# One product of 512 columns, which nobody reads, ahead of each group of transposes in a kernel of chunked attention and routed feed-forward

## The chip, the cores and the metric

The kernel runs on one core of a Trainium2 chip. The metric is the device time of one execution in microseconds; several executions are timed, and their median counts. One more execution is recorded by the hardware profiler. The engines are named as in the profile: PE is TensorE's matmul, PEld its loading of weights, DVE is VectorE, ACT is ScalarE, POOL is GpSimd and SP is SyncE, which issues DMAs.

## The reference

Two stages follow each other. The first is attention in chunks of 32 rows over a sequence of 768, for 4 batches of 8 heads with 64 features each. A chunk sees its own 32 keys, 16 to the left, 8 to the right, and 8 keys of a memory:

```python
for c in range(nc):                      # 24 chunks of 32
    q_c   = q[:, :, c_start:c_end]
    k_ctx = k[:, :, max(0, c_start - 16):min(S, c_end + 8)]
    k_full = np.concatenate([mem_k, k_ctx], axis=2)     # v_full alike
    scores = scale * np.matmul(q_c, k_full.transpose(0, 1, 3, 2))
    a = softmax(scores)
    out[:, :, c_start:c_end] = np.matmul(a, v_full)
```

The second takes the heads side by side as 512 features. For each batch it picks the 128 rows of 768 with the highest `x @ w_gate`, and adds a gated feed-forward result to these rows alone:

```python
top_idx = np.argpartition(-scores[b], capacity)[:capacity]
xe = x[b, top_idx]
ye = np.maximum(xe @ w1, 0.0) @ w2
out[b, top_idx] = x[b, top_idx] + g[:, None] * ye       # g: sigmoid of the scores
```

## The kernel before

The work is cut into 16 pairs of heads (4 for each batch) and 4 batches of routing. Each piece is a step with a name, a number and an engine: `TK.3.p` is step TK of pair 3 on TensorE (`p`), `.v` is VectorE, `.a` ScalarE, `.g` GpSimd, `.s` SyncE. The string ORDER at the top of the file lists all steps in one order, written out by hand; the last loop of the kernel walks through it and issues them. Each engine carries out its own steps in that order and waits by semaphores for what a step needs. There is no scheduler behind it.

The steps of a pair, as far as they are spoken of here:

- LK, LQ, LV (line 141) load K, Q and V of a pair from memory, with a cast from float32 to float16, as DMAs that GpSimd issues. MK and MV (lines 157 and 163) copy the rows of the memory keys and values in, from SyncE; those of pair 0 come from GpSimd (155, 161). Six buffers for each of K, Q and V go round, so the load of pair n + 6 waits until the transposes of pair n have read theirs.
- TK, TQ and TV (function `tr`, line 269) transpose these tiles on TensorE: 16 products for each step, into one PSUM bank. Four banks (pool `prr`) go round for all steps that use `bank16` or `bank32`. There are 16 x 3 = 48 of these groups.
- EK, EQ, EV (copies at lines 127 to 131) bring the result to kT, qT and vT; FK, FV and VP complete them.
- W0 and W1 (lines 319 and 329) transpose windows of V; S (378) makes the scores, R (390) their maximum, A (395) subtracts it by a product with a negative identity, E (402) takes the exponential, PT (410) transposes it, PV (441) multiplies with V, and RC, GP and NM (460, 464, 470) normalise. LW loads the weights of the feed-forward, ST (478) stores a batch of attention's output.

The routing of a batch follows when its four pairs are done: the steps with an m, such as mSC, mB, mC and mT (ranking by comparisons), mGI (a gather by DMA, line 601), mF (first product, 632), mY (second product, 662 and 667, with 512 columns each), and mSCAT (a scatter with addition, line 679). For the last batch, products with a selection matrix (617) take the place of the gather.

The first steps of TensorE in ORDER are TK.0, TQ.0, TV.0, S.0, A.0, TQ.1, TV.1, TK.1, TK.2, W0.0, W1.0, TV.2, PT.0, S.1. The identity that the transposes use, `ident16`, is made by VectorE at line 205, `rot16` at 206 and 207.

Of the kernel before, what the change touches and what calls it, by code (L numbers as in the profile page):

```python
# [8 lines left out]
FP = mybir.dt.float32  # L9
# [71 lines left out]
def kernel(  # L81
# [13 lines left out]
    nc = tc.nc  # L95
# [85 lines left out]
    ident16 = cst.tile([128, 128], F16, tag="ident16")  # L181
# [70 lines left out]
    def bank16(name):  # L252
        return prr.tile([128, 1024], F16, tag="r", name=name)
# [8 lines left out]
    pr_ = [St() for _ in range(NPR)]  # L262
    EARLY = NPR - NP

    def tr(n, src, rows, perm, name):
        p = bank16(name)
        for j in range(8):
            for h in range(2):
                nc.tensor.transpose(out=p[64 * h:64 * h + 64, rows * j:rows * j + rows],  # L269
                                    in_=src[n % GB][0:rows, h, 64 * j:64 * j + 64],  # L270
                                    identity=perm)
        return p

    def TQ(n, e):
        pr_[n].pq = tr(n, qls, 96, ident16[0:96, 0:96], "p_q")

    def TK(n, e):
        pr_[n].pk = tr(n, kls, R, rot16, "p_k")

    def TV(n, e):  # L280
        pr_[n].pv = tr(n, vls, R, rot16, "p_v")
# [417 lines left out]
    for token in ORDER.split():  # L699
        name, n, e = token.split(".")  # L700
# [36 lines left out]
```

## Time and profile before

| what | value |
|---|---|
| median of 3 runs | 152.33 us (151.75 to 153.22) |
| profiled execution | 150.89 us |
| its span, from the first instruction to the last | 149.2 us |
| PE busy | 110.2 us (74%), 2920 matmuls |
| PEld busy | 90.3 us (61%), 2920 weight loads |
| DVE busy | 94.2 us (63%) |
| ACT busy | 84.6 us (57%) |
| POOL busy | 66.2 us (44%) |
| mean granted clock of TensorE | 0.878 of full speed |
| moved by DMA | 20.51 MB |

Times are counted from the start of the span. Ends of matmuls are modelled, so the busy share of PE is an upper figure. A row of the view by windows reads: the window, its length in us; then for PE, PEld, DVE, ACT and POOL the busy us with the number of instructions in brackets; then the granted clock as a share of full speed, the mean busy share of the 16 DMA engines (over 1 where packets overlap on an engine), and GB/s. Asked for one line of the kernel, the view has PE and PEld alone. A row of the timeline reads: start and length in us, engine, line, operation, what it writes and reads, how many; in square brackets the idle time of the engine before it and what ended that.

### The profile page before, as it was taken

How to read it: one execution, taken by the hardware profiler on the slowest of the kernel's cores; microseconds unless marked ns; L12 is line 12 of the kernel's file. 1: busy time of each engine (PE TensorE's matmuls, PEld its weight loads, DVE VectorE, ACT ScalarE, POOL GpSimd, SP SyncE). 2: the span in 40 equal slices, each digit the busy share in tenths (PEclk: the TensorE clock that was granted, in tenths of full speed). 3: DMA queues.
4: the chain of work that ended last, by engine and by line, in shares of the span. 5: the costliest groups of instructions: out<-in, count | busy, mean ns of one | idle time of the engine just before them, and what ended most of it. 6: DMA issues, size and time to landing. Idle time of an engine off the chain costs nothing.

```text
span 149.2 us, 6550 instructions
## 1 busy us (share of the span) xinstructions
PE 110.2 (74%) x2920; PEld 90.3 (61%) x2920; DVE 94.2 (63%) x207; ACT 84.6 (57%) x139; POOL 66.2 (44%) x119
## 2 busy tenths in 40 slices
PE   0344199984877929697599989989999987799400
PEld 0332198863655819586487867877889676669100
DVE  0771245897169894395447999789798795964000
ACT  3830067973469784606647957979895783412300
POOL 6799069289059591355834014115126027204120
PEclk9999999999599985555559999999999999969975
DMA  2969967969999999999999910501930022365450
GB/s 16 143 69 182 201 107 111 140 90 153 194 180 159 155 286 285 227 209 205 204 242 265 325 38 4 75 4 23 352 130 4 0 77 18 57 255 182 62 70 0
DMA packets 17084, 20.51 MB, mean 137 GB/s; under 512 B 2324, under 2 KB 12564, under 8 KB 17056
## 3 DMA queue, kind: packets, MB, share of 16 engines
q0 software_dynamic: 12832, 13.55, 58.0%
q1 hardware_dynamic: 4224, 6.54, 12.4%
q8 instruction: 23, 0.38, 0.9%
q14 instruction: 5, 0.04, 0.1%
HBM read 24.21 MB, written 7.34 MB: 211 GB/s over the span
## 4 chain that ended last, share of the span: by engine, by line
PE 49%; DMA 15%; issue 15%; DVE 9%; ACT 3%; POOL 3%; POOLq 1%; ACTq 0%; SPq 0%
DMA out_dram<-y,idx 6%; PE p_x L441 5%; PE p_k L269 5%; PE p_v L269 4%; PE p_w L319 4%; PE p_s L378 4%; DMA vl<-mv 4%; PE p_s L395 4%; PE p_v L319 4%; PE p_p L410 4%; PE p_q L269 3%; DMA mv<-in_mem_v_dram 3%; PE p_h L632 3%; DVE m L390 2%; PE p_v L329 2%
## 5 line engine op out<-in xcount | busy, mean ns | idle before, releaser
L127 ACT COPY vT<-p_v 128x800 f16<-128x800 f16 x15 | 12.2, 828 | 14.1 <-PE p_v L269 14.0
L402 ACT ACTIVATE P<-p_s 128x768 f16<-128x768 f32 x16 | 13.0, 815 | 9.6 <-PE p_s L395 7.4
L390 DVE TENSOR_REDUCE m<-p_s 128x12 bf16<-128x768 f32 x16 | 15.2, 952 | 5.1 <-PE p_s L378 5.1
L441 PE MATMUL p_x<-vw,pt 128*64 128x66 f16 (+2 forms) x480 | 12.7, 202 | 4.5 <-issue 1.6
L470 DVE TENSOR_TENSOR x<-p_x,rd 128x768 f32<-128x768 f32 x16 | 15.2, 950 | 0.6 <-PE p_x L441 0.4
L319 PEld LDWEIGHTS <-vT 128*128 128x128 f16 x192 | 13.7, 109 | 2.7 <-issue 0.8
L131 POOL COPY vT<-vT 128x576 f16<-128x576 f16 (+1 forms) x14 | 7.9, 570 | 16.8 <-ACT vT L127 13.6
L441 PEld LDWEIGHTS <-pt 128*64 128x64 f16 x480 | 10.6, 121 | 7.4 <-issue 3.6
L269 PE MATMUL p_k<-rot,kl 100*64 100x100 f16 x256 | 10.8, 243 | 5.6 <-DVE vl L199 5.6
L536 DVE TENSOR_SCALAR cmp<-brow,scr 128x768 f16<-128x768 f32 x24 | 14.3, 642 | 0.5 <-ACT brow L127 0.5
L679 POOL DMA_INDIRECT out_dram<-y,idx x4 | 6.5, 1627 | 17.6 <-ACT y L673 7.5
L378 PE MATMUL p_s<-kT,qT 64*32 64x64 f16 x768 | 9.6, 206 | 6.1 <-issue 4.9
L127 ACT COPY qT<-p_q 128x768 f16<-128x768 f16 x12 | 9.6, 803 | 7.6 <-PE p_q L269 7.6
L269 PE MATMUL p_v<-rot,vl 100*64 100x100 f16 x256 | 10.7, 239 | 4.1 <-DMA vl<-mv 3.3
L269 PE MATMUL p_q<-ident,ql 96*64 96x96 f16 x256 | 10.2, 231 | 4.7 <-issue 2.6
L269 PEld LDWEIGHTS <-kl 100*64 100x64 f16 x256 | 8.7, 135 | 6.4 <-DMA kl<-in_k_dram 5.6
L129 DVE COPY pt<-p_p 64x768 f16<-64x768 f16 x19 | 10.5, 552 | 2.9 <-POOL ltri L242 2.0
L141 POOL DMA_DIRECT2D kl<-in_k_dram x16 | 10.5, 657 | 4.0 <-DMA vl<-in_v_dram 1.3
L378 PEld LDWEIGHTS <-qT 64*32 64x32 f16 x768 | 7.1, 95 | 8.4 <-issue 6.0
L141 POOL DMA_DIRECT2D ql<-in_q_dram x16 | 10.3, 646 | 4.1 <-DMA w_sb<-in_moe_w_dram 2.7
L269 PEld LDWEIGHTS <-ql 96*64 96x64 f16 x256 | 7.9, 126 | 7.0 <-issue 3.6
L269 PEld LDWEIGHTS <-vl 100*64 100x64 f16 x256 | 8.3, 130 | 5.9 <-issue 4.6
(103 smaller groups left out, 253.7 us busy)
## 6 DMA issues: line engine op xcount, KB each, us to landing
out_dram<-x SPq DMA_DIRECT2D x24, 256.0 KB
kl<-in_k_dram POOLq DMA_DIRECT2D x16, 192.0 KB, 7.5
ql<-in_q_dram POOLq DMA_DIRECT2D x16, 192.0 KB, 7.4
vl<-in_v_dram POOLq DMA_DIRECT2D x16, 192.0 KB, 7.2
w_sb<-in_moe_w_dram POOLq DMA_DIRECT2D x8, 256.0 KB, 9.5
vl<-mv SPq DMA_DIRECT2D x15, 8.0 KB
kl<-mk SPq DMA_DIRECT2D x15, 8.0 KB
mk<-in_mem_k_dram POOLq DMA_DIRECT2D x1, 128.0 KB, 5.2
```

The source lines that it names most:

```text
L127: nc.scalar.copy(out=out, in_=in_)
L129: nc.vector.tensor_copy(out=out, in_=in_)
L131: nc.gpsimd.tensor_copy(out=out, in_=in_)
L141: nc.gpsimd.dma_start(out=dst[n % GB][p0:p0 + 96, :, :], in_=_dap(src, 2 * n * HD, [[512, 96], [HD, 2], [1, 512]]))
L269: nc.tensor.transpose(out=p[64 * h:64 * h + 64, rows * j:rows * j + rows], in_=src[n % GB][0:rows, h, 64 * j:64 * j + 64], identity=perm)
L319: nc.tensor.transpose(out=p.bitcast(F16)[:, 128 * o:128 * o + 128], in_=pair(n, 6 * i + o), identity=ident16)
L378: nc.tensor.matmul(out=s.s[32 * c:32 * c + 32, h, 64 * blk:64 * blk + 64], lhsT=qf[64 * h:64 * h + 64, 32 * ch:32 * ch + 32], rhs=kf[64 * ...
L390: nc.vector.tensor_reduce(out=s.m, in_=keys(s.s), axis=AX.X, op=ALU.max)
L402: nc.scalar.activation(out=s.P, in_=keys(s.s), func=AF.Exp, scale=0.125)
L441: nc.tensor.matmul(out=X[64 * cc:64 * cc + 64, c2, w * (2 * bp + h):w * (2 * bp + h) + w], lhsT=s.PT[:, i, c, :, :].rearrange("p b t -> p ...
L470: nc.vector.tensor_tensor(out=x5.rearrange("p b g (h d) -> p b g h d", d=D), in0=s.x[:, :, :, :, 0:64], in1=s.rd.unsqueeze(4).to_broadcast ...
L536: (nc.vector if e == DVE else nc.gpsimd).tensor_scalar(out=t, in0=m.brow, scalar1=m.scr[:, bl:bl + 1], scalar2=None, op0=ALU.is_lt)
```

## The change

`tr`, which all 48 groups of transposes go through, takes its PSUM bank and then, before its first transpose, issues a product of the 128 x 128 identity with the identity repeated four times: 128 rows, 128 weight columns, 512 columns out in float32, which fill the bank. The transposes then write the same bank, and nothing reads the product. Ahead of the first group, TK.0, there are eight such products instead of one. These 55 products, each with its weight load, are all that is added to TensorE; the other engines' instructions and ORDER are the same.

```diff
+    def idle(p, times):
+
+        for _ in range(times):
+            nc.tensor.matmul(out=p.bitcast(FP)[:, 0:512], lhsT=ident16, rhs=ident16.unsqueeze(1).to_broadcast([128, 4, 128]),
+                             start=True, stop=True, skip_group_check=True)
+
     def tr(n, src, rows, perm, name):
         p = bank16(name)
+        idle(p, 8 if name == "p_k" and n == 0 else 1)
         for j in range(8):
             for h in range(2):
                 nc.tensor.transpose(out=p[64 * h:64 * h + 64, rows * j:rows * j + rows],
```

## Prediction

> **What bounds the kernel now.** I read the page first, for the clock and the DMA in slices:
>
> ```profile
> span 149.2 us, 6550 instructions
> PE   0344199984877929697599989989999987799400
> PEclk9999999999599985555559999999999999969975
> DMA  2969967969999999999999910501930022365450
> q8 instruction: 23, 0.38, 0.9%
> ```
>
> Each slice is 3.73 us. The granted TensorE clock is half in slice 11 and from slice 16 to 21, and in that part of the span, from slice 10 to 23, the 16 DMA engines are full. The last line counts 23 packets that fetch instructions.
>
> The second view is the chain of waits. Its pieces named "issue" are times in which an engine waited for nothing that the profile shows (columns: start, length in us). These, of the stretch 35 to 87 us, are the long ones; each is an idle TensorE between two instructions of one group:
>
> ```profile
> 35.29 2.59 issue
> 42.82 1.07 issue
> 47.76 1.02 issue
> 53.16 2.82 issue
> 61.22 1.14 issue
> 67.94 0.61 issue
> 73.09 1.57 issue
> 85.80 0.48 issue
> ```
>
> The third view cuts the span where these pieces end (PE and PEld counts in brackets):
>
> ```profile
> 37.88:43.89 6.01, 4.94 (x128) 3.73 (x127) 2.37 (x5) 4.11 (x6) 1.37 (x4) 0.73 1.20 199
> 43.89:48.78 4.89, 3.66 (x128) 2.99 (x128) 4.14 (x10) 4.05 (x7) 4.60 (x8) 1.00 1.01 152
> 48.78:55.98 7.20, 4.38 (x127) 3.75 (x128) 6.70 (x12) 5.46 (x10) 5.41 (x10) 0.92 1.11 223
> 55.98:62.36 6.38, 5.24 (x128) 4.62 (x128) 3.00 (x8) 3.27 (x6) 1.26 (x2) 0.50 1.17 265
> 62.36:68.55 6.19, 5.33 (x128) 4.44 (x129) 4.33 (x9) 2.74 (x6) 3.15 (x5) 0.50 1.24 208
> 68.55:74.66 6.11, 4.43 (x127) 3.71 (x127) 3.20 (x8) 3.28 (x5) 4.32 (x6) 0.50 1.24 204
> 74.66:80.43 5.77, 5.67 (x126) 4.61 (x127) 3.07 (x8) 3.09 (x5) 1.30 (x3) 0.65 1.21 233
> 80.43:86.27 5.84, 5.37 (x127) 4.62 (x127) 5.38 (x10) 5.05 (x11) 1.77 (x4) 1.00 1.02 309
> ```
>
> The reader is to see the counts. Every piece holds 253 to 257 TensorE instructions, at full clock and at half clock alike, and ends with a stop. With 23 fetch packets for some 5,890 TensorE instructions (256 each), I read this as TensorE waiting for its own code: while the DMA engines are full (share 1.0 to 1.24), a block of 256 takes 4.9 to 7.2 us, mean 48.39 / 8 = 6.05, whatever TensorE does meanwhile. From 35 to 86 us the rate of code is the bound, about 24 ns for each instruction.
>
> The fourth view takes stages, then the same for the transposes' line alone:
>
> ```profile
> 18.20:24.09 5.89, 5.87 (x136) 5.34 (x136) 1.71 (x3) 3.23 (x5) 3.99 (x11) 1.00 0.70 121
> 24.09:35.17 11.08, 10.41 (x376) 8.78 (x361) 10.44 (x22) 9.62 (x15) 7.77 (x18) 1.00 0.83 117
> 86.27:119.39 33.12, 32.22 (x1002) 26.51 (x1002) 28.26 (x65) 26.29 (x44) 8.79 (x15) 1.00 0.24 69
> ...
> 35.17:86.27 51.10, 12.09 (x288) 9.90 (x287) 0.73 1.15 222
> 86.27:119.39 33.12, 7.70 (x240) 5.94 (x240) 1.00 0.24 69
> ```
>
> From 18.2 to 24 us and again from 86 to 119 us TensorE itself is the bound (5.87 of 5.89 and 32.22 of 33.12 us busy); in between VectorE has 10.44 of 11.08. After 119 us come the chains of the last routing and the scatters, with no group of transposes in them.
>
> **The change part by part.** 48 groups (16 pairs, K, Q and V) get one product of 512 columns each, the first gets eight: 55 products, which with their weight loads are 110 more TensorE instructions. The instruction lists of VectorE, ScalarE, GpSimd and SyncE, with their DMAs, keep their length and order, so nothing is moved past a queue. The new product takes the bank that its group takes anyway, so it adds no bank and waits for the same release; only what is queued behind it on TensorE comes later.
>
> Price of one product, from the only groups with 512 columns (start, length of the group):
>
> ```profile
> 87.85 1.04 PE L662 MATMUL p_y<-w_sb,hT 128*128 128x512 f16 x4
> 88.82 0.57 PE L441 MATMUL p_x<-vw,pt 128*64 128x66 f16 x24
> 132.01 1.66 PE L662 MATMUL p_y<-w_sb,hT 128*128 128x512 f16 x4
> ```
>
> At full clock the next group starts 0.97 us after four of them: 0.24 us each at most. I take 0.23. In a stretch at half clock it is 1.66 / 4 = 0.42.
>
> *Up to 18.2 us.* The rows that decide:
>
> ```profile
> 4.32 0.23 DVE L205 CAST ident<-ident 128x128 f16<-128x128 f32 x1 [4.32 <-POOL ident masks.py:199]
> 5.62 0.88 PE L269 MATMUL p_k<-rot,kl 100*64 100x100 f16 x16 [5.62 <-DVE vl L199]
> 14.06 0.85 PE L269 MATMUL p_q<-ident,ql 96*64 96x96 f16 x16 [1.61 <-DMA ql<-in_q_dram]
> 18.22 0.88 PE L269 MATMUL p_v<-rot,vl 100*64 100x100 f16 x16 [3.30 <-DMA vl<-mv]
> 24.70 0.53 PE L269 MATMUL p_q<-ident,ql 96*64 96x96 f16 x16
> ```
>
> A group takes 0.85 to 0.88 here and 0.53 after 24.1 us, so the clock is half up to there, though the view of windows prints 1.00 ahead of its first record. Eight products can start when the identity is there (4.55) and end near 4.7 + 8 x 0.42 = 8.1, so the first group starts 2.5 us late. Four more (ahead of TQ.0, TV.0, TQ.1, TV.1) make 12 x 0.42 = 5.0 us, against 0.9 us of idle time before 5.62 and waits of 1.61 and 3.30 us that a DMA ends: 5.8. I cost it at nothing; the cover is DMA waiting. If it is gone, what does not fit is paid in full, 2.5 us for the eight.
>
> *18.2 to 35.2 us.* The clock between its changes:
>
> ```profile
> 24.09:37.75 13.66, 10.54 (x376) 8.78 (x361) 11.64 (x24) 9.62 (x15) 9.96 (x21) 1.00 0.88 124
> 37.75:41.16 3.41, 3.28 (x61) 2.47 (x61) 0.78 (x2) 2.00 (x4) 0.00 (x0) 0.50 1.20 198
> 54.81:78.71 23.90, 19.05 (x452) 16.04 (x453) 13.73 (x33) 11.37 (x18) 11.05 (x17) 0.50 1.21 231
> ```
>
> Three products at half clock (TK.1, TK.2, TV.2) lie on TensorE's path: 1.26 us. Seven more at 0.23 are 1.6, of which I count a quarter, 0.4, because VectorE is nearly full there too and the next block of code is then late anyway. Against it a gain: full clock is granted from 24.09 on, and the grant changes in steps of 3.41 us (one from 37.75 to 41.16, four before it, seven in 23.90). More work in the array may bring it one step sooner: 3.41 x 0.4 = 1.4 us less, with 0.4 the share that a group saves (0.88 to 0.53). Bounds: -1.0 (products hidden) to +2.9 (no gain); I take 1.26 + 0.4 - 1.4 = +0.3, between the two, as either is open.
>
> *35.2 to 86.3 us.* Each product itself lies in a time that is spent on waiting for code; 18 groups (x288 / 16) are two a block, 0.5 to 0.9 us, where most stops are longer. It costs nothing. But it adds two instructions, and by the last of these boundaries the stream has 33 x 2 + 14 = 80 more. TensorE stands 80 instructions further back: 80 / 256 x 6.05 = 1.9 us. I take 1.5, since the block 74.66 to 80.43 was busy throughout at half clock and may win a little. Bounds: 0 (fetching quickens as the loads, which follow TensorE by their buffers, come later) and 3.1 (one more block of 1.2 us delay at the end of the crowded part).
>
> Here the clock may well recover, and I cost that at nothing. In 37.88 to 43.89 at a mean of 0.73, 43.89 to 48.78 at 1.00 and 55.98 to 74.66 at 0.50, the block stays near 6 us; a faster TensorE only stops longer. The Trainium skill, "Runtime: NRT & Kernel Launch", section "Instruction fetch mechanics", says that code comes in blocks of 256 instructions over DMA and that crossing a boundary is mostly hidden. The trace agrees with the size (253 to 257) and not with the hiding (eight stops, 11.3 us); by that rule the stage would go at TensorE's pace, which is the first rival below.
>
> *86.3 to 119.4 us.* x240 / 16 = 15 groups, 15 x 0.23 = 3.45 us on a TensorE that idles 0.9 us in 33.1. I take 2.9: a product ahead of a group hides only where TensorE waits. Bounds: 2.0 (VectorE, 28.26 of 33.12 us busy, sets part of the pace) and 3.6.
>
> *After 119.4 us.* No product. The work moves later as a whole: 0, with -1.5 to +2 for where a short half-clock stretch falls in the last routing.
>
> Sum: 0 + 0.3 + 1.5 + 2.9 + 0 = +4.7 us. The profiled execution took 150.89 us (span 149.2), 1.44 below the median of the runs shown, so it gives 155.6 for its like; the runs should give 152.33 + 4.7 = 157.0.
>
> **The rivals.** *Faster: the clock pays.* If code is fetched by position and not by time, 35 to 86 us goes at TensorE's pace. From 54.81 to 78.71 at half clock it was busy for 19.05 us. At full clock that is 0.4 x 19.05 = 7.6 us less, and 0.4 x 3.28 = 1.3 for 37.75 to 41.16. Against it stand 0.3 and 2.9 from above, and 18 products x 0.23 = 4.1 in this stage, half of it in stops: -8.9 + 5.3 = -3.6, or 148.7. For it: the stops at 35.29 and 53.16 us, the longest two, stand just before the two falls of the clock (37.75 and 54.81). Against it: the constant count and nearly constant length of the blocks. It decides once the eight blocks together lose more than the 4.7 us of the sum, 0.6 each, and so shrink below 5.45. The Trainium skill, "TensorE: Matmul & The Clock Gate", part 1, says that an idle window of about 3.4 us halves the clock and a busy one restores it, which speaks for the change's power over the clock; the steps of 3.41 us agree.
>
> *Mostly covered.* The extra code costs nothing and VectorE's pace hides a third of the late products: 0.3 + 0 + 2.0 = +2.3, or 154.6, at best +1.
>
> *The start overflows.* The first group's delay reaches the loads that GpSimd issues behind its first copies, and a load that stands ready now comes late: 2.5 us and up to 2 more after 119 us, 4.7 + 2.5 + 2 = +9.2, or 161.5.
>
> *It does not do what it says:* the clock still falls. Then only the 1.4 us are missing: +6.1, or 158.4. This lies in my forecast's range.
>
> **How the numbers follow.** Forecast 0.62 (its own range 155.0 to 160.0), mostly covered 0.17, faster 0.14, overflow 0.07. A measurement of this kernel tells about 1%, 1.5 us, from no change. Faster by over 1%: 0.12 of the 0.14. Within 1%: the other 0.02 and 0.05 of "mostly covered". Slower: 0.81. The range leaves out the faster rival and the far end of the overflow: 153.0 to 160.5.
>
> **What would show it.** Right: cutting the span of the changed kernel at its long "issue" pieces again gives 256 instructions and about 6 us for each block from 35 to 87 us, with or without half clock; the first group starts near 8 us but TV.1's group still near 18.2; the last of the stops holds work that came 80 instructions earlier before; the stretch with the last 15 groups is about 3 us longer. Wrong: blocks that shorten when the clock is full, or a stretch after 86 us that grows by less than 1.5 us.

## The result, and the profile after

The changed kernel takes 158.27 us (median of 4 runs, 156.97 to 160.85) against 152.73 us before (4 runs on the same chip): a ratio of 1.041, with a 95% interval of 1.033 to 1.049. Some executions of a kernel are a few per cent slower than its others, and each ratio here and below leaves such executions out, so it is not the quotient of the two medians beside it, which take in all. The forecast was 157.0 us in a range of 153.0 to 160.5, slower. The profiled execution took 156.97 us against 150.89, its span is 155.3 us against 149.2: +6.1.

The head of the page after:

```profile
span 155.3 us, 6659 instructions
PE   0894299985899967889789699989999995999500
PEclk9999759999779995557999999999999997599985
DMA  2969956949997999999999911401930011518540
```

In the middle the clock is half in three slices (16 to 18) instead of six (16 to 21), so in this execution the clock is held up more, and the kernel is slower all the same. The long "issue" pieces of the chain of waits after, between 35 and 88 us (start, length):

```profile
37.15 2.08 issue
54.83 1.35 issue
61.41 1.19 issue
73.78 1.08 issue
80.30 0.60 issue
85.67 1.35 issue
```

The span after, cut where TensorE starts a new block of 256 instructions (counts of PE and PEld in brackets, granted clock third from the end):

```profile
39.22:45.57 6.35, 6.35 (x125) 4.38 (x128) 3.07 (x6) 2.89 (x5) 0.76 (x2) 0.73 1.20 199
45.57:50.10 4.53, 4.34 (x144) 3.08 (x144) 3.54 (x9) 4.12 (x6) 4.04 (x8) 1.00 0.71 110
50.10:56.17 6.07, 4.72 (x134) 3.63 (x130) 5.66 (x12) 4.43 (x8) 4.90 (x9) 1.00 1.10 175
56.17:62.59 6.42, 4.68 (x127) 3.82 (x128) 3.63 (x6) 4.14 (x8) 2.52 (x5) 0.65 1.14 286
62.59:68.89 6.30, 5.73 (x128) 4.61 (x128) 3.33 (x10) 2.35 (x4) 2.72 (x5) 0.50 1.23 215
68.89:74.86 5.97, 4.89 (x130) 3.44 (x129) 4.61 (x10) 3.66 (x6) 3.16 (x5) 0.76 1.24 206
74.86:80.90 6.04, 5.44 (x127) 3.86 (x126) 4.08 (x10) 4.10 (x6) 3.72 (x5) 1.00 1.21 227
80.90:87.03 6.13, 4.78 (x128) 3.42 (x128) 4.53 (x8) 3.46 (x9) 1.78 (x4) 1.00 1.15 282
```

These are the blocks of before within a fraction of a microsecond: together 47.81 us against 48.39. (Where TensorE does not stop at a cut, an instruction that runs across it is counted on both sides, as in the second of these rows, where they add up to 288; the eight blocks in one row hold 1017 and 1017:

```profile
39.22:87.03 47.81, 40.93 (x1017) 30.23 (x1017) 32.46 (x69) 29.16 (x49) 23.60 (x40) 0.82 1.14 216
```

and before it was 1016 and 1016 in 48.39 us.) In the last two the clock is full, where before it was half for most of the first of them, and they take 6.04 and 6.13 us instead of 5.77 and 5.84. A faster TensorE stops longer and no more.

The traces also hold the packets that fetch this code, one for each block. In the kernel before, the packet for the next block starts 2.6 to 4.6 us after a block is entered in the stretch of full DMA engines (37.9 to 80.4 us), and 0.0 to 1.2 us after it between 86 and 115 us, where they have room. At each of the eight stops listed for it, TensorE goes on 1.3 to 1.7 us after this packet has ended. In all fourteen traces of this study together, 71 stops of over 0.4 us between 35 and 92 us stand whole multiples of 256 instructions apart in their own kernel, when the waits in TensorE's queue, which the rows by windows leave out, are counted too; after each of them TensorE goes on 1.2 to 1.7 us after the end of the packet. So it is its code that TensorE waits for at these stops.

Rows of the timeline after that fix where the time went (start, length, engine, line):

```profile
4.61 3.59 PE L268 MATMUL p_k<-ident 128*128 128x512 f16 x8 [4.61 <-DVE ident L205]
8.13 0.88 PE L276 MATMUL p_k<-rot,kl 100*64 100x100 f16 x16
18.47 0.88 PE L276 MATMUL p_v<-rot,vl 100*64 100x100 f16 x16 [3.35 <-DMA vl<-mv]
83.50 0.53 PE L276 MATMUL p_q<-ident,ql 96*64 96x96 f16 x16
93.56 0.54 PE L276 MATMUL p_k<-rot,kl 100*64 100x100 f16 x16
121.04 0.55 PE L276 MATMUL p_k<-rot,kl 100*64 100x100 f16 x16
```

and the last three of these groups (TQ.10, TK.11, TK.15) before:

```profile
81.68 0.51 PE L269 MATMUL p_q<-ident,ql 96*64 96x96 f16 x16
90.62 0.54 PE L269 MATMUL p_k<-rot,kl 100*64 100x100 f16 x16
114.86 0.54 PE L269 MATMUL p_k<-rot,kl 100*64 100x100 f16 x16
```

The loss grows along the kernel: +0.25 us at TV.1 (18.47), +1.8 at TQ.10, +2.9 at TK.11, +6.2 at TK.15, and after that nothing more (34.3 us from there to the end of the span before, 34.2 after).

### The profile page after: what moved, and what is told of

It is laid out like the page before. It is cut to its first block, busy times and chain, and to the rows that moved or that the text cites. A ratio compares the mean times of both kernels' runs of the same rounds, so it can differ in the third digit from the quotient of the medians.

```text
span 155.3 us, 6659 instructions
## 1 busy us (share of the span) xinstructions
PE 124.2 (80%) x2975; PEld 92.2 (59%) x2975; DVE 94.8 (61%) x207; ACT 85.3 (55%) x139; POOL 66.1 (43%) x119
## 4 chain that ended last, share of the span: by engine, by line
PE 72%; issue 7%; DMA 7%; ACT 3%; DVE 3%; POOL 2%; POOLq 1%
PE p_x L448 7%; PE p_k L276 6%; PE p_k L268 6%; PE p_q L276 5%; PE p_v L276 5%; PE p_v L326 5%; PE p_w L326 5%; PE p_s L402 4%; PE p_s L385 4%; PE p_p L417 4%; PE p_h L639 4%; DMA vl<-mv 4%; DMA out_dram<-y,idx 3%; PE p_v L336 3%; PE p_q L268 3%
## 5 line engine op out<-in xcount | busy, mean ns | idle before, releaser
L326 PEld LDWEIGHTS <-vT 128*128 128x128 f16 x192 | 13.1, 106 | 3.3 <-issue 0.7
L448 PEld LDWEIGHTS <-pt 128*64 128x64 f16 x480 | 11.1, 124 | 5.7 <-issue 2.6
L268 PE MATMUL p_k<-ident 128*128 128x512 f16 x23 | 10.2, 505 | 4.6 <-DVE ident L205 4.6
L276 PE MATMUL p_v<-rot,vl 100*64 100x100 f16 x256 | 9.4, 220 | 3.3 <-DMA vl<-mv 3.3
L127 ACT COPY pt<-p_p 64x768 f16<-64x768 f16 x13 | 10.3, 793 | 2.7 <-PE p_p L417 2.3
L276 PEld LDWEIGHTS <-vl 100*64 100x64 f16 x256 | 7.1, 116 | 7.8 <-issue 7.6
L141 POOL DMA_DIRECT2D vl<-in_v_dram x16 | 10.3, 645 | 2.9 <-DMA ql<-in_q_dram 1.3
L127 ACT COPY kT<-p_k 128x800 f16<-128x800 f16 x11 | 9.1, 825 | 4.1 <-PE p_k L276 4.1
L276 PEld LDWEIGHTS <-kl 100*64 100x64 f16 x256 | 7.9, 126 | 5.5 <-issue 4.7
L276 PEld LDWEIGHTS <-ql 96*64 96x64 f16 x256 | 6.9, 116 | 6.7 <-issue 5.8
```

Source lines behind the costliest of these rows:

```text
L127: nc.scalar.copy(out=out, in_=in_)
L141: nc.gpsimd.dma_start(out=dst[n % GB][p0:p0 + 96, :, :], in_=_dap(src, 2 * n * HD, [[512, 96], [HD, 2], [1, 512]]))
L268: nc.tensor.matmul(out=p.bitcast(FP)[:, 0:512], lhsT=ident16, rhs=ident16.unsqueeze(1).to_broadcast([128, 4, 128]), start=True, stop=True, ...
L326: nc.tensor.transpose(out=p.bitcast(F16)[:, 128 * o:128 * o + 128], in_=pair(n, 6 * i + o), identity=ident16)
L448: nc.tensor.matmul(out=X[64 * cc:64 * cc + 64, c2, w * (2 * bp + h):w * (2 * bp + h) + w], lhsT=s.PT[:, i, c, :, :].rearrange("p b t -> p ...
```

## The experiments

The theory: from 35 to 87 us TensorE is paced by the arrival of its code, 256 instructions in about 6 us, because the DMA engines are full; there a product costs only through its two instructions. After 87 us TensorE is the bound and a product costs its time in the array (the part of its time that grows with its columns). The rivals: each product costs its length wherever it stands; or the clock matters and its recovery pays.

**Parts of the change.** Eight products ahead of the first group alone:

```diff
-        idle(p, 8 if name == "p_k" and n == 0 else 1)
+        if name == "p_k" and n == 0:
+            idle(p, 8)
```

> Eight products ahead of the first group, none elsewhere. Theory (the first eight are covered by DMA waiting; later only their 16 instructions count, 16 x 24 ns): +0.4 us, TV.1's group still near 18.3 us. Rival (the late start is carried through): +2.5 us, TV.1's group near 20.7.

Measured: 152.40 us against 153.82, ratio 1.013 (0.999 to 1.027): no difference that this can tell, and TV.1's group starts at 18.09 us, so the start is covered up to there. Next, the first 33 groups and the last 15 apart (LATE holds the names of the last 15):

```diff
-        idle(p, 8 if name == "p_k" and n == 0 else 1)
+        if ("T" + name[-1].upper(), n) not in LATE:
+            idle(p, 8 if name == "p_k" and n == 0 else 1)
```

> Products ahead of the first 33 groups only (eight ahead of the first), none ahead of the last 15. Theory (code is the bound from 35 to 87 us): the boundaries of the blocks of 256 as in the changed kernel within 0.5 us, +1.5 to +2.0 us in all. Rival (the clock pays and only the last products cost): a gain, -1 to -4 us. Rival (every product costs its own length, 29 x 0.3 us): +9 us.

Measured: 156.40 us, ratio 1.038 (1.024 to 1.052), some 5.7 us and more than expected. The eight blocks keep their length (49.08 us, shown below), but the first begins at 36.90 us and not at 39.22 as in the changed kernel, and the boundaries lie 0.6 to 2.3 us ahead of that kernel's, where 0.5 was expected. TK.11 starts at 92.30 us, 1.7 later than before, as the theory has it. Of the other 3.0 us by which the span of this profile (153.9) is longer than before, 1.3 are lost where no product stands, in a stop for code that before does not have; the rest has no single place that the trace shows:

```profile
109.00:111.00 2.00, 2.00 (x56) 1.81 (x54) 1.80 (x5) 1.49 (x3) 0.41 (x2) 1.00 1.01 378
```

```profile
111.70 0.32 PE L452 MATMUL p_x<-vw,pt 128*64 128x64 f16 x8
113.34 0.44 PE L452 MATMUL p_x<-vw,pt 128*64 128x64 f16 x16 [1.32 <-issue]
```

The store of a batch, issued from 107.01 us on, fills the DMA engines (share 1.01 from 109 us on), and the block whose fetch fell into it is 1.3 us late: its packet starts 3.72 us after the block ahead of it was entered at 107.36. Before, the same store was issued from 104.76 us on, the block that ends at this boundary was entered at 107.55, and the packet started 0.66 us after that. That the 80 instructions more moved the boundary to the head of the store is how I read this; it was not tried apart. The clock's rival, a gain, is out: here the clock was full for more of the stage than in any other run with all loads (0.90, below).

```diff
-        idle(p, 8 if name == "p_k" and n == 0 else 1)
+        if ("T" + name[-1].upper(), n) in LATE:
+            idle(p, 1)
```

> Products ahead of the last 15 groups only. Theory (TensorE is the bound there, 0.31 us from a product's start to the transposes behind it in the changed kernel): 15 x 0.29 = +4.4 us and nothing ahead of 90 us. By the price of the prediction, 0.23 with some hidden: +2.9 us. Rival (VectorE sets the pace): under +2 us.

Measured: 155.59 us, ratio 1.033 (1.020 to 1.046). The first and the last of its groups:

```profile
90.17 0.54 PE L280 MATMUL p_k<-rot,kl 100*64 100x100 f16 x16
117.78 0.54 PE L280 MATMUL p_k<-rot,kl 100*64 100x100 f16 x16
```

From TK.11 to TK.15 it takes 27.61 us against 24.24 before: 3.4 us for 14 products, 0.24 each. (The run with the eight first products alone, which has none here, takes 24.93; against that it is 0.19 each.) VectorE does not hide them. My expectation of 0.29 each was too high: it was read from a product's start to the next group's start, and part of that is there for a product of any size, as the next runs show.

The first 33 groups and the last 15 (3.8% and 3.3%) add up to more than the whole change (4.1%). The seven runs of the kernel before that stood beside them lie between 149.91 and 154.59 us, and the eight products alone read 1.3% there, so these ratios are no prices to within a per cent. The prices are those read from the stages of the traces.

**The same instructions, other columns.** All 55 products with 8 columns, and, in a kernel of its own, each as four of 128 (the two edits one below the other):

```diff
-            nc.tensor.matmul(out=p.bitcast(FP)[:, 0:512], lhsT=ident16, rhs=ident16.unsqueeze(1).to_broadcast([128, 4, 128]),
+            nc.tensor.matmul(out=p.bitcast(FP)[:, 0:8], lhsT=ident16, rhs=ident16[:, 0:8],
...
+            for i in range(4):
+                nc.tensor.matmul(out=p.bitcast(FP)[:, 128 * i:128 * i + 128], lhsT=ident16, rhs=ident16,
```

> All 55 products with 8 columns instead of 512: as many instructions, almost no time in the array. Theory (in 35 to 87 us an instruction costs by being fetched): the group TQ.10 +1.5 us, then 15 x 0.08 = +1.2, in all +2.7 us. Rival (a product costs its time in the array): +0.5 to +1 us.

Measured: 158.66 us, ratio 1.045 (1.028 to 1.062), as much as the whole change, though the array has almost nothing to do for it. TQ.10 starts 2.7 us later than before, where 1.5 was expected:

```profile
84.38 0.53 PE L276 MATMUL p_q<-ident,ql 96*64 96x96 f16 x16
```

(Three executions with nothing added ahead of this group have it at 81.36 to 82.06, so a single one tells it to within 0.7 us.) Then there is a stop for code of 1.06 us, and 2.6 us after it the clock falls for three steps in a stretch where TensorE has no idle time left:

```profile
101.89 0.37 PE L276 MATMUL p_k<-rot,kl 100*64 100x100 f16 x8 [1.06 <-issue]
```

```profile
104.50:114.80 10.30, 10.30 (x242) 8.83 (x227) 6.41 (x14) 7.26 (x12) 2.38 (x4) 0.50 0.51 178
```

So this run alone could not tell a product's price after 87 us. The last run of the study asks it again, with 8 columns ahead of the last 15 groups only:

```diff
+        if ("T" + name[-1].upper(), n) in LATE:
+            idle(p, 1)                               # with [:, 0:8] as above
```

> Products of 8 columns ahead of the last 15 groups only: 30 instructions, almost no time in the array. Theory (in that stretch a product costs its time in the array, and the 8-column run of all groups lost more there by a stop for code and the half clock that followed): +0.5 to +1 us, TK.11 to TK.15 under 25.3 us. Rival (a product costs its instructions or the change of weights, whatever its columns): +3 to +4.5 us, TK.11 to TK.15 near 27.4 us.

Measured: 154.43 us against 154.08, ratio 1.003 (0.998 to 1.009); TK.11 to TK.15:

```profile
90.95 0.54 PE L280 MATMUL p_k<-rot,kl 100*64 100x100 f16 x16
116.65 0.54 PE L280 MATMUL p_k<-rot,kl 100*64 100x100 f16 x16
```

25.70 us, 1.46 more than before, 0.10 each, a little over the 25.3 expected. After 87 us a product costs its time in the array, 0.14 of 0.24 us, and at most 0.1 for being there (0.05 against the 24.93 us of the run with the eight products alone).

> Each product of 512 columns as four of 128, the same columns in all but four times the instructions (440 more than before). Theory (code is the bound from 35 to 87 us, about 24 ns an instruction): the blocks of 256 still take about 6 us there, the group TQ.10 starts some 8 us later than before instead of 1.8, in all +12 us. Rival (a product costs its time in the array): as the changed kernel within 1 us, +5 to +6.5.

Measured: 159.86 us against 151.57, ratio 1.044 (1.031 to 1.056). The blocks keep their length, with 440 more instructions in the stream; eight blocks in a row, from boundary to boundary, in this run, in the run with products ahead of the first 33 groups, and in that with 8 columns:

```profile
35.35:84.91 49.56, 40.87 (x1023) 33.31 (x1023) 29.74 (x66) 27.78 (x45) 25.61 (x42) 0.76 1.15 204
```

```profile
36.90:85.98 49.08, 39.08 (x1016) 28.91 (x1016) 32.70 (x69) 28.89 (x49) 24.13 (x41) 0.90 1.14 213
```

```profile
36.91:87.30 50.39, 41.30 (x1017) 34.06 (x1017) 32.37 (x69) 29.26 (x49) 24.53 (x41) 0.70 1.14 217
```

These 2,032 to 2,046 instructions take 47.8 to 50.4 us in all of these executions, at mean clocks from 0.70 to 0.90 and with quite different work in them. With four times the instructions, TQ.10 starts 5.4 us later than before and 3.6 later than after the change, though the columns are the change's:

```profile
87.07 0.53 PE L277 MATMUL p_q<-ident,ql 96*64 96x96 f16 x16
```

That is the theory's sign and not the rival's, but not the 8 us expected: the first of the eight blocks began 2.5 us sooner in this execution than before (35.35 against 37.88). The whole time does not tell the two apart: by the ratio it lost 6.6 us, about as much as the change (1.044 and 1.041), which is the rival's figure and far from the 12 us expected.

**Where the code is late, and what it hides.** Two thirds of the bytes of the loads of pairs 6 to 15 are left out:

```diff
-        nc.gpsimd.dma_start(out=dst[n % GB][p0:p0 + 96, :, :],
-                            in_=_dap(src, 2 * n * HD, [[512, 96], [HD, 2], [1, 512]]))
+        r = 96 if n < GB else 32
+        nc.gpsimd.dma_start(out=dst[n % GB][p0:p0 + r, :, :],
+                            in_=_dap(src, 2 * n * HD, [[512, r], [HD, 2], [1, 512]]))
```

> No products; the loads of pairs 6 to 15 bring 32 of the 96 rows (two thirds of these loads' bytes are left out, and the old rows stay in the buffers). Theory (code comes late because the DMA engines are full): from about 50 us on the stops shrink or vanish, the blocks take 4 to 5 us, in all -5 to -9 us. Rival (the stops have nothing to do with the loads): blocks of 6 us, within 1 us of before.

Measured: 143.70 us against 151.57, ratio 0.945 (0.937 to 0.954).

```profile
38.50:78.18 39.68, 35.58 (x1017) 29.42 (x1017) 31.34 (x67) 30.61 (x52) 20.89 (x39) 0.83 0.85 176
```

The same eight blocks take 39.68 us instead of 48.39, at a DMA share of 0.85. TensorE's instructions are those of before, so it is the loads that make the code late. The clock (0.83 against 0.73) is not the reason: at 0.90 and with all loads, in the run with the first 33 groups, the eight blocks took 49.08 us.

The same, with the change's products as well:

```diff
+        idle(p, 8 if name == "p_k" and n == 0 else 1)
```

> The lighter loads of the run before with the change's 55 products. Theory (with code in time the products lie on TensorE's path from 50 us on as well): more lost against the light loads alone than the change loses, +6.5 to +10 us. Rival (clock): with code in time the recovered clock pays, less lost than +5.5.

Measured: 151.98 us, ratio to the same before 0.992 (0.981 to 1.003). Against the light loads alone that is 4.7% of the time before, 7.1 us, where the change costs 4.1%, 6.3 us. This lies in the theory's range, but the two differ by less than their intervals, so it is not shown that the products of the middle lie on TensorE's path once code is in time. What it does show is that no recovered clock pays for them.

**Less code.** If code is the bound, fewer instructions should gain. The source has a second form of the scores that takes both heads in one product (24 products instead of 48 for a pair), with two copies that lay out the queries. It was switched on for some pairs, with the copies' steps added to ORDER and no products:

```diff
-    QBS = set(())
+    QBS = {4, 5, 6, 7, 9}
```

> No products; the scores of pairs 4, 5, 6, 7 and 9 with both heads in one product (24 products with 128 rows instead of 48 with 64, a way that the source has; queries are laid out for it by two copies on GpSimd for each pair). 240 TensorE instructions fewer, all before 82 us. Theory (code): up to 240 x 24 ns = 5.7 us less, -3 to -5.5 in all. Rival (time in the array and the copies count): 0 to +2 us.

Measured: 154.93 us, ratio 1.024 (1.017 to 1.032): slower. The timeline says why; TK.10 and the scores of pair 9 behind it, and GpSimd's copy:

```profile
72.41 0.52 PE L266 MATMUL p_k<-rot,kl 100*64 100x100 f16 x16
...
80.85 0.83 POOL L128 COPY qb<-qT 64x768 f16<-64x768 f16 x1 [6.58 <-DMA xg<-out_dram,idx]
...
81.73 0.85 PE L364 MATMUL p_s<-kT,qb 128*64 128x64 f16 x24 [7.26 <-POOL qb L128]
```

Before, TK.10 was here:

```profile
77.26 0.87 PE L269 MATMUL p_k<-rot,kl 100*64 100x100 f16 x16
```

So 192 instructions fewer (those of pairs 4 to 7; the scores of pair 9 come behind it) brought TensorE 4.85 us ahead there, 25 ns each. Then the second copy of pair 9 stood on GpSimd's queue behind a gather for 6.6 us, and TensorE waited 7.3 us for it. Three more versions, run beside each other:

```diff
+    QBS = {4, 5, 6, 7}              # copies QB0 and QB1 on GpSimd
...
+    QBS = {4, 5, 6, 7, 9}           # QB0.9 on ScalarE, QB1.9 on VectorE
...
+    QBS = {2, 3, 4, 5, 6, 7}        # copies on GpSimd
```

> As the run with less code, but pair 9 as before, since there a copy on GpSimd stood behind a gather for 6.6 us: pairs 4 to 7, 192 instructions fewer. Theory (code): 192 x 24 ns = 4.5 us earlier by TK.10, at the end -2 to -4.5 us, and better than before. Rival (code is not what counts, or the copies on GpSimd hold up loads): within 1 us of before or slower.

> Pairs 4 to 7 as in the run beside it, and pair 9 with its two copies on ScalarE and VectorE, 240 instructions fewer. Theory (code): TK.10 up to 4.5 us earlier, TK.11 up to 5.5, -3 to -5 us at the end. Rival (the gather or the two copies hold TensorE up again): no better than the run beside it.

> Pairs 2 to 7, 288 instructions fewer, copies on GpSimd. Theory (code): boundaries of the blocks after 35 us at the same times, TK.10 up to 6.5 us earlier, -3 to -6 us. Rival (the copies of pairs 2 and 3 hold up the loads on GpSimd's queue, or TensorE waits for them): slower than the run with pairs 4 to 7.

Measured, against 153.60 us: pairs 4 to 7 give 154.69, ratio 1.008 (1.004 to 1.012); with pair 9 on ScalarE and VectorE 152.59, ratio 0.987 (0.981 to 0.994); pairs 2 to 7 155.97, ratio 1.010 (1.004 to 1.016). The second is faster than the kernel before, by 1.3% (by 0.7% if the medians of all executions are taken), less than expected; the other two miss. At TK.10 they are 3.0 and 1.7 us ahead of before and, with pairs 2 to 7, 0.9 behind, where 4.5, 4.5 and 6.5 ahead were expected. In all three the copies on GpSimd hold up its copies of vT, and TensorE waits 3.4 to 3.7 us for those; here with pairs 4 to 7:

```profile
57.52 0.68 POOL L128 COPY vT<-vT 128x576 f16<-128x576 f16 x1
...
58.25 0.82 PE L316 MATMUL p_w<-ident,vT 128*128 128x128 f16 x6 [3.44 <-POOL vT L128]
```

The second has this wait too:

```profile
57.58 0.82 PE L316 MATMUL p_w<-ident,vT 128*128 128x128 f16 x6 [3.44 <-POOL vT L128]
```

So the wait does not set the first apart from the second. That one loses its lead behind TK.10, with two stops for code (0.92 and 0.84 us) and a wait of 0.98 us for a gather: its TK.11 starts at 91.26 us, 0.6 later than before, and the second's at 89.29, 1.3 earlier. While TensorE waits for GpSimd its blocks take longer than 6 us, up to 9.2 in these two, without a stop for code, so these runs are no clean test of the rate of code. The price of less code was a longer queue on another engine.

## Why the prediction was right

The sign, the range and the cause hold: 158.27 us lies in 153.0 to 160.5, and the blocks keep the length that they were said to keep. The sum itself was 1.4 us short. By its own terms, against the profiled execution (+6.1 where +4.7 was summed):

- *Up to 18.2 us, 0.* Right. Eight products end and the first group starts at 8.13 us (8.1 forecast), TV.1's at 18.47 (18.22 before), and the eight alone change nothing that can be measured.
- *18.2 to 35.2 us, +0.3.* Too small: the block that began at 31.92 begins at 33.47, +1.5. From TV.1 to TV.2 the three products at half clock cost 1.7 us, where 1.26 was said; the ones behind them cost nothing more up to that block; the gain of 1.4 us from an earlier clock did not come. How much of the +1.5 is the change's stays open: the run with the first 33 groups has the same products up to there and began this block at 31.60. The eight products raised the clock within 6 us, and in the wait for TV.1 it fell again:

```profile
10.28:17.11 6.83, 2.95 (x87) 1.68 (x85) 2.99 (x4) 0.98 (x2) 4.50 (x8) 1.00 1.14 180
17.11:23.94 6.83, 5.38 (x75) 4.02 (x75) 1.55 (x2) 2.36 (x3) 3.37 (x8) 0.50 0.82 138
```

  Full clock came at 23.94 us, against 24.09. Two other runs agree that work ahead of such a wait buys nothing behind it: full clock came at 22.11 us in the run with the products of the first 33 groups, and at 22.18 in the run with the last 15 alone, which has none up to there. The Trainium skill ("TensorE: Matmul & The Clock Gate", part 1) says that a busy window of about 3.4 us raises the clock and an idle one lowers it. The trace agrees: the clock rose at 10.28 us and fell at 17.11, two steps of 3.41 us later, in the wait of 3.35 us before TV.1.
- *35.2 to 86.3 us, +1.5.* The mechanism is right and shown by the fetch packets and by the run with lighter loads; with four times the instructions the place of TQ.10 bears it out, the whole time does not. The late start of the stage was made up on the way (+1.3 us at the first boundary, +0.8 at the last), 80 more instructions left TQ.10 1.8 us late, and the last stop before TK.11, 1.35 us where it was 0.48, adds most of another microsecond: with the term above +2.9 in all at TK.11, of which 0.2 is that group's own product, where 0.3 + 1.5 + 0.2 was forecast. Without the term above and that product, this stage is +1.2 where +1.5 was forecast.
- *86.3 to 119.4 us, +2.9.* TK.11 to TK.15 takes 27.48 us instead of 24.24: 3.24 us for 14 products, 0.23 each, the price that was taken from the rows of 512 columns. The deduction for hiding, half a microsecond, was wrong: nothing hides them.
- *After 119.4 us, 0.* Right (34.3 and 34.2 us to the end).

So the shortfall of 1.4 us is 1.2 in the second term, where the clock's gain did not come, and 0.6 in the fourth, where nothing was hidden, less 0.3 in the third. The rival that the change does not do what it says had 158.4, nearest of all to what was measured, but by luck: its condition, that the clock still falls as before, did not hold in this trace; only the gain that it leaves out failed to come.

The rival that the clock pays did not come about: half clock lasts from 58.07 to 71.72 instead of 54.81 to 78.71 us, ten microseconds less, and the eight blocks together are 0.6 us shorter. (One execution does not show how far that is the products' doing: from 35 to 87 us, three runs with no product there have 20.5 to 27.3 us of half clock, the changed kernel 17.1, the run with the first 33 groups 10.2, and the one with four products of 128 columns 23.9.) Where the DMA engines had room, TensorE did not stop at a boundary: the kernel before has no such stop after 87 us, and the lighter loads, at a share of 0.85, took 8.7 us off the same eight blocks. The Trainium skill ("Runtime: NRT & Kernel Launch", "Instruction fetch mechanics") says that crossing a block of code is mostly hidden. The trace of the kernel before agrees after 87 us, where the DMA engines have room, and not from 35 to 87 us, where they are full.

What stays open: how much of each run's loss after 87 us is where the block boundaries happen to fall against stores and gathers. Four executions show such stops of 0.45 to 1.32 us (at 112 and 101 us, as shown, and at 99 and 116 us in the runs with less code in pairs 4 to 7 and 2 to 7); their cause beyond the crowded DMA in the first was not tried.

## What to carry to other kernels

Ahead of working on TensorE's clock, cut the span at its unexplained stops and count instructions between them: if the count is always the same, look whether code is the bound. Here it was, and a faster clock did not shorten the blocks; fewer bytes on the DMA engines did, while fewer instructions brought 1.3% at best. A filler product is free only where the engine waits for something else, and each must be priced in the stage where it stands: here 0.24 us on TensorE's path, nothing that could be measured ahead of a DMA, two instructions where code is late. What takes work off one engine's code puts it on another's queue, so look there for the next wait before the gain is counted.

## What the runs showed that was not expected

Products of 8 columns in all groups cost as much as those of 512 (ratio 1.045 against 1.041), with a stop for code of 1.06 us and then half clock for 10.3 us in a full stretch, while the same products ahead of the last 15 groups alone cost nothing that can be measured (1.003). And stops for code appear outside the crowded stage as well: 1.3 us at 112 us, with a store on the DMA engines, in a kernel whose only change lies before 85 us.
